# Splitting the attention's score products into quarters, preparing the first block of the next layer during the attention, and reordering the last rows

## The chip, the core and the metric

The kernel runs on one core of a Trainium2 chip. The metric is the device time of one launch in microseconds (us), and the median over several runs is compared.

A core has several engines that run at the same time, each with a queue of its own that it works off strictly in order: PE (TensorE, the matrix products, with its weight loads shown as PEld), DVE (VectorE), ACT (ScalarE), POOL (GpSimd) and SP (SyncE, which here only issues DMA transfers). They wait for each other by semaphores. PE writes its results to a small memory, PSUM, from which DVE or ACT must take them before the place can be written again.

## What is computed

Three layers in a row. The attention has 4 batches and 8 heads, a sequence of 576 and a head dimension of 64; scores that lie more than `tau` below the largest of their row are dropped. Then come two dense layers on 2304 tokens:

```python
scores = scale * np.matmul(q, k.transpose(0, 1, 3, 2))
thresh = np.max(scores, axis=-1, keepdims=True) - tau
scores = np.where(scores >= thresh, scores, -1000000000.0)
attn = exp(scores - max);  attn = attn / (sum(attn) + 1e-09)
x = matmul(attn, v)                       # heads side by side: 2304 x 512
x = ((x @ w_a) * (x @ w_b)) @ w_out       # 512 -> 1536 -> 512
h = x @ w_in                              # 512 -> 1024
solu = h * softmax(h);  ln = (solu - mean) / sqrt(var + 1e-06) * g_ln
out = ln @ w_out2                         # 1024 -> 512
```

## The kernel before

**Order by hand.** The program is written under a manual schedule: each engine gets its instructions in the order in which the Python code emits them, and semaphores are added for every dependence. So the place of a line in the code is its place in its engine's queue.

**Attention (lines 236 to 510).** The 8 heads of each batch are taken in pairs: 16 pairs. A pair has 9 sets of 128 rows of scores (`NS`): 8 full ones and one that holds the last 64 rows of both heads. One step of the loop over `m` (line 430) does two sets, so there are 72 steps with new sets and 6 more that empty the pipeline. In a step the letters of `PROG` give the order. `A` and `B` compute one set each: the products on PE (`scores`, line 280), the row maximum on DVE (line 293) and the exponential on ACT (line 305). `V` multiplies earlier, already transposed weights with `v` (`pv`, line 361). `F` ends a pair. `T`, `U` and `Y` transpose the two sets of the step before on PE (lines 339, 355, 358), and their copies out of PSUM are put at the end of the step on ACT. `a` and `b` mask the two sets on DVE (line 319), and `f` and `z` are places at which small leftover operations go to DVE: reciprocals, and the conversion of weights for the next layer (`conv_emit`), which goes on at every even `m` and at every `m` from 72.

A set has K = 64 (the head dimension). Its 576 columns are cut into two halves `g`, one in the upper 64 rows of the array and one in the lower, so that the two products run side by side. Each f32 product is issued as two passes. A full set is 4 matmul instructions, with 128 columns of weights each. The set of the last 64 rows is 8 instructions on quarters of the array (64 rows by 64 columns).

**The next layer (`moe1`, line 527).** The 2304 tokens are cut into 5 blocks: 4 of 512 tokens, one a batch, and one of 256. A unit is a pair of a block `j` and a slice `f` of 128 hidden columns: `ab` (line 538) computes 24 products of 512 columns into a `ps` buffer, of which there are two, and takes them out by ACT (line 555) and DVE (line 556). Two units later `yacc` adds 12 products. Between the units stand the weight conversion and the preparation of the next block.

**Preparation of a block.** `load_x` (line 182) issues the transfers of the attention's output `xr`, of the reciprocals `zr` and of the small `vs`. `prep_x` (line 197) with `st=0` normalises by four instructions of 512 columns on DVE (line 210) and copies the high part by two of 1024 columns on ACT (line 211); with `st=1` it subtracts to get the low part by two of 1024 columns on DVE (line 213) and orders the store `xsd` (line 215). For block 0 `load_x` stands at `m` = 62, and `prep_x` at the head of the steps 71 and 72 (lines 431 to 434), in front of their scores.

**The last layer (`moe2`, line 638).** 18 tiles of 128 tokens. `hid` (line 649) does 24 products and then a chain over DVE, ACT and POOL (lines 660 to 677) whose result `e` is transposed by `lnt` (line 682): 8 transposes on PE, then twice a multiplication on DVE (line 693), a copy of the high part on ACT (line 694) and a subtraction for the low part (line 695), which is on POOL but for the last tile. `outp` (line 700) does 24 products on the result. In the last step (t = 17) the code emits `hid(17)`, `lnt(16)`, `outp(15)`, the first half of `outp(16)`, `lnt(17)`, the rest of `outp(16)` and `outp(17)`.

Of the kernel before, what the change touches and what calls it, by code (L numbers as in the profile page):

```python
# [8 lines left out]
F32 = mybir.dt.float32  # L9
# [4 lines left out]
AF = mybir.ActivationFunctionType  # L14
ALU = mybir.AluOpType
AX = mybir.AxisListType
PSUM = bass.MemoryType.PSUM
P = 128
# [3 lines left out]
def kernel(  # L22
# [65 lines left out]
    xs = {}  # L88
    vs = {}
    vnew = []  # L90
    later = []
    xhs = [xh_p, None]
    wst = {}
# [88 lines left out]
    def load_x(j):  # L182
        n = LEN[j]
        xr = xr_p.tile([P, KC, NB], F32, name="xr0")[:, :, 0:n]
        zr = xr_p.tile([P, KC, NB], F32, name="zr")[:, :, 0:n]
        for b, s0, m, c in BLK[j]:
            nc.sync.dma_start(out=xr[:, :, c:c + m], in_=xd[b][:, :, s0:s0 + m])
            if b not in vs:
                vs[b] = xr_p.tile([P, KC, 2], F32, name="vs", bufs=B)
                nc.sync.dma_start(out=vs[b], in_=xd[b][:, :, S:S + 2])  # L190
                vnew.append(b)
            for h in range(2):
                zs = rzd[b].rearrange("(k h) s -> h k s", h=2)[h:h + 1, :, s0:s0 + m]
                nc.sync.dma_start(out=zr[h * D:(h + 1) * D, :, c:c + m], in_=zs.to_broadcast([D, KC, m]))
        xs[j] = (xr, zr, xhs[j % 2].tile([P, KC, 2, NB], F32R, name="xt")[:, :, :, 0:n])

    def prep_x(j, st):
        xr, zr, xt = xs[j]
        if st == 0:
            while vnew:  # L200
                b = vnew.pop()
                nc.vector.tensor_scalar(out=vs[b], in0=vs[b], scalar1=neg, scalar2=EPS / S, op0=ALU.mult, op1=ALU.mult)
        for c in range(0, KC, 2):
            k = slice(c, c + 2)
            x0 = xr[:, k]
            if st == 0:
                for e in range(c, c + 2):
                    for b, _, m, o in BLK[j]:
                        xe = xr[:, e, o:o + m]
                        nc.vector.scalar_tensor_tensor(out=xe, in0=xe, scalar=vs[b][:, e, 0:1], in1=zr[:, e, o:o + m], op0=ALU.add, op1=ALU.mult)  # L210
                nc.scalar.activation(out=xt[:, k, 0, :], in_=x0, func=AF.Copy)
            else:
                nc.vector.tensor_tensor(out=xt[:, k, 1, :], in0=x0, in1=xt[:, k, 0, :].bitcast(F32), op=ALU.subtract)
        if st == 1:
            later.append(lambda: nc.sync.dma_start(out=xsd[j], in_=xr))
            xs[j] = xt

    def load_x2(j):
        n = LEN[j]
# [16 lines left out]
    def attention():  # L236
# [43 lines left out]
        def scores(i, s):  # L280
            q, k = ld[i]
            ps = ps_s.tile([P, 2, 512], F32, name="ps")
            qc, h = divmod(s, 2)
            parts = [(slice(0, P), h, slice(qc * P, (qc + 1) * P), 0)] if s < 2 * NQ else [(slice(u * D, (u + 1) * D), u, slice(SM, S), u * D) for u in range(2)]
            for rows, u, c, o in parts:
                for g in range(2):
                    r = slice(g * D, (g + 1) * D)
                    nc.tensor.matmul(ps[rows, g, 0:HS], lhsT=q[r, u, c], rhs=k[r, u, o:o + HS], start=True, stop=True, skip_group_check=True)  # L288
            st[i, s] = ps

        def soft_max(i, s, nm):
# [134 lines left out]
                        conv_emit(wstage, "APD", 2)  # L426

        conv_at = [x for x in range(6, tot // 2 + 6) if x % 2 == 0 or x >= tot // 2]
        PROG = 'ABtVFTUYaufbz'
        for m in range(tot // 2 + 6):  # L430
            if m == tot // 2 - 10:
                load_x(0)
            if 0 <= m - tot // 2 + 1 < 2:
                prep_x(0, m - tot // 2 + 1)
            cur = [divmod(n, NS) for n in (2 * m, 2 * m + 1) if n < tot]
            old = [divmod(n, NS) for n in (2 * m - 2, 2 * m - 1) if 0 <= n < tot]
            lo_old, lo_q = lo_q, []
            pvs = [(j,) + PV[j % 2][m - j * NS // 2] for j in range(max(0, 2 * m // NS - 2), min(NP, 2 * m // NS + 1)) if m - j * NS // 2 in PV[j % 2]]
            mms = [f for p in pvs for f in pv(*p)]
            nm = {}  # L440
            th = {}

            def score(k):
                if k < len(cur):
                    nm[k] = sm.tile([P, 1], F32, name="nm")
                    scores(*cur[k])
                    soft_max(*cur[k], nm[k])
                    soft_exp(*cur[k])

            def thr(k):  # L450
                if k < len(cur):
                    th[k] = soft_thr(nm[k])

            def mask(k):
                if k < len(cur):
                    soft_mask(*cur[k], th[k])
                    if cur[k][1] == NS - 1:
                        recip(cur[k][0])

            def turn(k):  # L460
                if k < len(old):
                    tpose(*old[k])

            for ch in PROG:
                if ch in "AB":
                    score("AB".index(ch))
                elif ch == "V":
                    for mm in mms:
                        mm()
                elif ch == "F":  # L470
                    for j in range(NP):
                        if m - j * NS // 2 == 9:
                            finish(j)
                elif ch in "TU":
                    turn("TU".index(ch))
                elif ch == "Y":
                    for c in old:
                        tpose_tail(*c)
                elif ch in "tu":
                    thr("tu".index(ch))  # L480
                elif ch in "ab":
                    mask("ab".index(ch))
                elif ch == "f":
                    fill(1)
                elif ch == "z":
                    fill(max(1, len(lo_old)))
            for fn in dma_q + later:
                fn()
            dma_q.clear()
            later.clear()  # L490
            i, s = divmod(2 * m, NS)
            r = m - (i * NS + 1) // 2
            if i < NP and r == 0:
                load_v(i)
                if i + 2 < NP:
                    alloc_qk(i + 2)
                    load_k(i + 2)
                    load_q(i + 2)
            for fn in pv_q + evac_q:
                fn()  # L500
            evac_q, pv_q = [], []
            if m in conv_at:
                conv_emit(wstage, "AP", 3)
                conv_load(wstage)
# [22 lines left out]
    def moe1(wp2, ps_t):  # L527
# [9 lines left out]

        def ab(j, f):
            n = LEN[j]
            xt = xs[j]  # L540
            wt = wst[f]
            ps = ps_s.tile([P, 2, 512], F32, name="ps")
            o = []
            for m in range(2):
                pa = ps[:, m]
                k = 0
                for kc in range(KC):
                    for wi, xi in ((0, 0), (0, 1), (1, 0)):
                        nc.tensor.matmul(pa[:, 0:n], lhsT=wt[:, m, wi, kc * P:(kc + 1) * P], rhs=xt[:, kc, xi, :], start=(k == 0), stop=(k == 3 * KC - 1))  # L549
                        k += 1  # L550
                o.append(pa[:, 0:n])
            a32 = gp.tile([P, NB], F32, name="a32")[:, 0:n]
            g32 = gp.tile([P, NB], F32, name="g32")[:, 0:n]
            gt = gp.tile([P, 2, NB], F32R, name="gt", bufs=2 + LAG)[:, :, 0:n]
# [83 lines left out]
    def moe2(ps_t):  # L638
# [7 lines left out]

        s1 = {}

        def hid(t):
            y = yt.pop(t)  # L650
            ph = ps_s.tile([P, 2, 512], F32, name="ps")
            for g in range(2):
                k = 0
                for kc in range(KC):
                    for a, b in ((0, 0), (0, 1), (1, 0)):
                        nc.tensor.matmul(ph[:, g, :], lhsT=y[:, a, kc, :], rhs=w2(2 * kc + g, b), start=(k == 0), stop=(k == 3 * KC - 1))  # L656
                        k += 1
            nm = sm.tile([P, 1], F32, name="nm")
            z = sm.tile([P, 3], F32, name="z2")
            nc.vector.tensor_reduce(out=nm, in_=ph, axis=AX.XY, op=ALU.max, negate=True)  # L660
# [21 lines left out]
        def lnt(t):  # L682
            c, rs = s1.pop(t)
            lt = xh_p.tile([P, 2, NJ, P], F32R, name="lt", tag="xt") if t % 2 else hp.tile([P, 2, NJ, P], F32R, name="lt", bufs=1)
            for g in range(2):
# [6 lines left out]
                l32 = wstage.tile([P, NJ // 2, P], F32, name="l32", tag="w32")  # L692
                nc.vector.tensor_tensor(out=l32, in0=pl, in1=gb, op=ALU.mult)  # L693
                nc.scalar.activation(out=lt[:, 0, gj], in_=l32, func=AF.Copy)  # L694
                (nc.vector if t == NTILE - 1 else nc.gpsimd).tensor_tensor(out=lt[:, 1, gj], in0=l32, in1=lt[:, 0, gj].bitcast(F32), op=ALU.subtract)  # L695
            s2[t] = (lt, rs)

        pos = {}
# [22 lines left out]
        for t in range(NTILE):  # L721
            if t + 2 < NTILE:
                load_y(t + 2, yp)
            if t + 1 < NTILE:
                split_y(t + 1, yp)
            hid(t)
            if t == NTILE - 1:
                lnt(t - 1)
            if 0 <= t - 2:
                outp(t - 2)  # L730
            if 0 <= t - 1 < NTILE - 2:
                lnt(t - 1)
# [76 lines left out]
```

## Time and profile before

| | |
|---|---|
| three runs | 959.18, 957.45, 958.80 us |
| median | 958.8 us |
| the profiled execution | 959.81 us, of which its span (first to last instruction) is 958.0 us |
| PE busy in the span | 938.0 us, 98% |
| DVE busy | 542.0 us, 57% |
| ACT busy | 441.3 us, 46% |
| POOL busy | 196.3 us, 20% |

A busy PE isn't PE at its best: the ends of its instructions are modelled, and one matmul in the pipeline overlaps the next. So gaps and distances between starts are read, not busy time. [...] In the timeline, equal instructions that follow one another are merged into one line. Its columns are: start, length, engine, line of the kernel, operation, result and operands, shape, count, and in brackets the idle time before it with what ended that. The attention covers about the first 278 us, `moe1` goes to about 732 us, and `moe2` to the end.

### The profile page before, as it was taken

To read this page: it belongs to the slowest core of one execution; us is meant where nothing else is said; L and a number is where in the kernel's file an instruction comes from. 1 tells how busy PE (TensorE), PEld (TensorE's weight loads), DVE (VectorE), ACT (ScalarE), POOL (GpSimd) and SP (SyncE) were. 2 spreads that over 40 slices of the span, in tenths; PEclk is the share of its full clock that TensorE was granted. 3 is DMA by queue.
4 is the path that set the end of the run, shared out by engine and by line. 5 is a ranking of instruction groups with operands and counts; after the bars stand their busy time and mean duration, and the time that the engine had idled before them with its cause. 6 is when DMAs were issued, how large, how long until landed. Compare 5 with 4: busy or idle time off the path is not lost.

```text
span 958.0 us, 14042 instructions
## 1 busy us (share of the span) xinstructions
PE 938.0 (98%) x5168; PEld 719.2 (75%) x5168; DVE 542.0 (57%) x1165; ACT 441.3 (46%) x793; POOL 196.3 (20%) x294
## 2 busy tenths in 40 slices
PE   7999999999999999999999999999999999999997
PEld 4656565665667888889888888889988788888885
DVE  6898989889975763223246762222265544444442
ACT  5788887888853451213225532111232433333332
POOL 1112221212221220000013420000022433333331
PEclk9999999999999999999999999999999999999999
DMA  6343343447245563133115541022062111111100
GB/s 176 120 127 112 122 140 102 120 128 199 71 136 154 182 205 75 61 94 132 45 44 199 182 169 67 24 87 78 11 198 66 34 45 44 44 45 44 44 23 34
DMA packets 52612, 95.39 MB, mean 100 GB/s; under 512 B 12736, under 2 KB 28736, under 8 KB 49984
## 3 DMA queue, kind: packets, MB, share of 16 engines
q1 hardware_dynamic: 52112, 93.91, 31.4%
q8 instruction: 41, 0.67, 0.3%
q10 hardware_dynamic: 432, 0.59, 0.2%
q14 instruction: 27, 0.22, 0.1%
HBM read 70.80 MB, written 23.68 MB: 99 GB/s over the span
## 4 chain that ended last, share of the span: by engine, by line
PE 66%; DVE 2%; DMA 2%; ACT 1%; POOL 0%; issue 0%; SPq 0%; ACTq 0%; DVEq 0%
PE ps L549 29%; PE py L572 15%; PE po L708 10%; PE ps L656 9%; PE pl L689 2%; DMA wraw<-in_w_dram 1%; DMA rzd<-zt 0%; POOL lt L695 0%; DVE e L664 0%; ACT e L663 0%; DVE nm L660 0%; ACT ps L668 0%; DVE g L556 0%; DVE e L667 0%; DVE l L693 0%
## 5 line engine op out<-in xcount | busy, mean ns | idle before, releaser
L549 PE MATMUL ps<-xt,w 128*128 128x512 f32 (+1 forms) x1440 | 311.6, 372 | 2.0 <-DVE g L556 2.0
L549 PEld LDWEIGHTS ps<-xt,w 128*128 128x128 f32 x1440 | 253.0, 189 | 51.9 <-DVE g L556 2.4
L144 POOL TENSOR_TENSOR w<-w,w 128x512 fp32r<-128x512 f32 x52 | 77.9, 1497 | 420.2 <-ACT w L141 420.2
L572 PE MATMUL py<-gt,w 128*128 128x512 f32 (+1 forms) x720 | 159.8, 371 | 0.0
L572 PEld LDWEIGHTS py<-gt,w 128*128 128x128 f32 x720 | 126.5, 188 | 24.7
L556 DVE TENSOR_TENSOR g<-ps,a 128x512 f32<-128x512 f32 (+1 forms) x60 | 38.2, 637 | 188.1 <-ACT a L555 188.1
L555 ACT ACTIVATE a<-ps 128x512 f32<-128x512 f32 (+1 forms) x60 | 33.2, 553 | 186.6 <-PE ps L549 183.4
L305 ACT ACTIVATE pe<-ns,nm 128x576 f32<-128x576 f32 x128 | 93.9, 774 | 48.3 <-DVE ns L293 48.1
L319 DVE SCALAR_TENSOR_TENSOR pe<-ns,th,pe 128x576 f32<-128x576 f32 x128 | 102.7, 815 | 16.3 <-ACT pe L305 12.5
L293 DVE TENSOR_SCALAR_CACHE_REDUCE ns<-ps 128x576 f32<-128x576 f32 x144 | 102.6, 749 | 10.7 <-PE ps L288 10.4
L708 PE MATMUL po<-w,lt 128*128 128x512 f32 x432 | 103.6, 395 | 2.7 <-ACT lt L694 1.4
L656 PE MATMUL ps<-w,ys 128*128 128x512 f32 x432 | 104.6, 397 | 1.5 <-POOL ys L524 1.4
L288 PE MATMUL ps<-k,q 64*128 64x288 f32 (+1 forms) x640 | 96.2, 439 | 5.0 <-DMA k<-in_qkv_dram 5.0
L708 PEld LDWEIGHTS po<-w,lt 128*128 128x128 f32 x432 | 81.7, 190 | 21.7 <-ACT lt L694 2.2
L656 PEld LDWEIGHTS ps<-w,ys 128*128 128x128 f32 x432 | 80.0, 188 | 19.6 <-POOL ys L524 1.8
L332 ACT ACTIVATE pt<-tp 128x512 f32<-128x512 f32 (+1 forms) x160 | 78.1, 545 | 1.7 <-PE tp L339 1.4
L310 POOL TENSOR_SCALAR th<-nm,toff 128x1 f32<-128x1 f32 x144 | 38.4, 268 | 188.0 <-DVE ns L293 188.0
L370 PE MATMUL po<-pt,vr 128*64 128x322 f32 (+1 forms) x512 | 76.6, 420 | 0.0
L339 PEld LDWEIGHTS tp<-ident,pe 128*128 128x128 f32 x512 | 56.4, 143 | 26.5 <-issue 14.4
L339 PE MATMUL tp<-ident,pe 128*128 128x128 f32 x512 | 71.6, 280 | 3.3 <-ACT pt L332 2.8
L288 PEld LDWEIGHTS ps<-k,q 64*128 64x128 f32 (+1 forms) x640 | 48.2, 178 | 30.2 <-issue 9.5
L660 DVE TENSOR_REDUCE nm<-ps 128x1 f32<-128x1024 f32 x18 | 22.0, 1224 | 70.0 <-PE ps L656 70.0
(72 smaller groups left out, 820.7 us busy)
## 6 DMA issues: line engine op xcount, KB each, us to landing
wraw<-in_w_dram SPq DMA_DIRECT2D x36, 512.0 KB
q<-in_qkv_dram SPq DMA_DIRECT2D x15, 576.0 KB
k<-in_qkv_dram SPq DMA_DIRECT2D x30, 176.0 KB
xd<-xp SPq DMA_DIRECT2D x16, 289.0 KB
y<-yd SPq DMA_DIRECT2D x18, 256.0 KB
vr<-in_v_dram SPq DMA_DIRECT2D x16, 256.0 KB
xr<-xd SPq DMA_DIRECT2D x4, 1024.0 KB
zr<-rzd SPq DMA_DIRECT2D x8, 512.0 KB
```

The source lines that it names most:

```text
L144: nc.gpsimd.tensor_tensor(out=w["o"][1], in0=w["f"] if wide else raw, in1=w["o"][0].bitcast(F32), op=ALU.subtract)
L288: nc.tensor.matmul(ps[rows, g, 0:HS], lhsT=q[r, u, c], rhs=k[r, u, o:o + HS], start=True, stop=True, skip_group_check=True)
L293: nc.vector.tensor_scalar(out=ns, in0=st[i, s][:, :, 0:HS], scalar1=-SCALE, scalar2=None, op0=ALU.mult, op1=ALU.min, accum_out=nm)
L305: nc.scalar.activation(out=pe.rearrange("p (g s) -> p g s", g=2), in_=ns, func=AF.Exp, bias=nm, scale=-1.0)
L319: nc.vector.scalar_tensor_tensor(out=pv, in0=ns, scalar=th, in1=pv, op0=ALU.is_le, op1=ALU.mult, accum_out=z[:, s:s + 1])
L332: evac_q.append(lambda: nc.scalar.activation(out=out, in_=in_, func=AF.Copy))
L339: nc.tensor.transpose(tp[:, kc, :], pe[:, o:o + P], ident)
L370: nc.tensor.matmul(po[h * D:(h + 1) * D], lhsT=lhsT, rhs=rhs, start=(kc == 0), stop=(kc == NQ), skip_group_check=True)
L549: nc.tensor.matmul(pa[:, 0:n], lhsT=wt[:, m, wi, kc * P:(kc + 1) * P], rhs=xt[:, kc, xi, :], start=(k == 0), stop=(k == 3 * KC - 1))
L572: nc.tensor.matmul(py, lhsT=wt[:, 2, wi, oc * P:(oc + 1) * P], rhs=gt[:, gi, :], start=(first and k == 0), stop=(last and k == 2))
L656: nc.tensor.matmul(ph[:, g, :], lhsT=y[:, a, kc, :], rhs=w2(2 * kc + g, b), start=(k == 0), stop=(k == 3 * KC - 1))
L708: nc.tensor.matmul(po, lhsT=lt[:, a, j, :], rhs=w2(2 * KC + j, b), start=(k == 0), stop=(k == 3 * NJ - 1))
```

## The change

- `scores`: a full set is no longer 2 products with 128 columns of weights in two passes, but 4 with 64 columns each, on quarters of the array, as the set of the last rows was before.
- `load_x(0)` is emitted at `m` = 30 instead of 62. `prep_x(0, ...)` is no longer called at `m` = 71 and 72. In its place `prep_slots` cuts the same work into pieces of 512 columns (4 norms, 4 high parts, 4 low parts) in 8 slots, and one slot is emitted at `z`, after the second mask, of each odd `m` from 37 to 51. The ACT part goes to the end of the list of copies of that step. `vs` moves to another pool.
- The products of `ab(0, 0)` are emitted at `m` = 72 after `Y` (`X` in `PROG`), in front of the last products with `v`. Their way out of PSUM stays in `moe1`.
- `moe2`: the DVE, ACT and POOL part of `hid` becomes `chain`, called after `hid(t)`, but in the last step only after `lnt(16)`. The low part of tile 16 goes to DVE, like that of tile 17.

```diff
@@ prep_slots, ab_mm (new) @@
+    def prep_slots(j):
+        xr, zr, xt = xs[j]
+        def norm(e):
+            while vnew:
+                b = vnew.pop()
+                nc.vector.tensor_scalar(out=vs[b], in0=vs[b], scalar1=neg, scalar2=EPS / S, op0=ALU.mult, op1=ALU.mult)
+            for b, _, m, o in BLK[j]:
+                xe = xr[:, e, o:o + m]
+                nc.vector.scalar_tensor_tensor(out=xe, in0=xe, scalar=vs[b][:, e, 0:1], in1=zr[:, e, o:o + m], op0=ALU.add, op1=ALU.mult)
+        def high(e):
+            nc.scalar.activation(out=xt[:, e, 0, :], in_=xr[:, e], func=AF.Copy)
+        def low(e):
+            nc.vector.tensor_tensor(out=xt[:, e, 1, :], in0=xr[:, e], in1=xt[:, e, 0, :].bitcast(F32), op=ALU.subtract)
+            if e == KC - 1:
+                later.append(lambda: nc.sync.dma_start(out=xsd[j], in_=xr))
+                xs[j] = xt
+        slots = []
+        for c in range(0, KC, 2):
+            slots += [(lambda e=e: norm(e), lambda e=e: high(e)) for e in range(c, c + 2)]
+            slots += [(lambda e=e: low(e), None) for e in range(c, c + 2)]
+        return slots
+    def ab_mm(j, f):
...
@@ scores @@
-            parts = [(slice(0, P), h, slice(qc * P, (qc + 1) * P), 0)] if s < 2 * NQ else [(slice(u * D, (u + 1) * D), u, slice(SM, S), u * D) for u in range(2)]
-            for rows, u, c, o in parts:
+            parts = [(h, qc * P + u * D, 0) for u in range(2)] if s < 2 * NQ else [(u, SM, u * D) for u in range(2)]
+            for t, (u, c0, o) in enumerate(parts):
+                c = slice(c0, c0 + D)
                 for g in range(2):
                     r = slice(g * D, (g + 1) * D)
-                    nc.tensor.matmul(ps[rows, g, 0:HS], lhsT=q[r, u, c], rhs=k[r, u, o:o + HS], start=True, stop=True, skip_group_check=True)
+                    nc.tensor.matmul(ps[t * D:(t + 1) * D, g, 0:HS], lhsT=q[r, u, c], rhs=k[r, u, o:o + HS], start=True, stop=True, skip_group_check=True)
@@ the loop over m @@
-        PROG = 'ABtVFTUYaufbz'
+        PROG = 'ABtVFTUYXaufbz'
-            if m == tot // 2 - 10:
+            if m == 30:
                 load_x(0)
-            if 0 <= m - tot // 2 + 1 < 2:
-                prep_x(0, m - tot // 2 + 1)
+                x_slots = prep_slots(0)
...
+                elif ch == "X":
+                    if m == tot // 2:
+                        pre[0, 0] = ab_mm(0, 0)
                 elif ch == "z":
                     fill(max(1, len(lo_old)))
+                    if m >= 37 and m % 2 and x_slots:
+                        norm_low, high = x_slots.pop(0)
+                        norm_low()
+                        if high:
+                            evac_q.append(high)
@@ ab @@
+            o = pre.pop((j, f)) if (j, f) in pre else ab_mm(j, f)
@@ moe2 @@
+            ph_of[t] = ph
+        def chain(t):
+            ph = ph_of.pop(t)
...
-                (nc.vector if t == NTILE - 1 else nc.gpsimd).tensor_tensor(out=lt[:, 1, gj], in0=l32, in1=lt[:, 0, gj].bitcast(F32), op=ALU.subtract)
+                (nc.vector if t >= NTILE - 2 else nc.gpsimd).tensor_tensor(out=lt[:, 1, gj], in0=l32, in1=lt[:, 0, gj].bitcast(F32), op=ALU.subtract)
...
             hid(t)
             if t == NTILE - 1:
                 lnt(t - 1)
+            chain(t)
```

## Rows read from the trace of the kernel before

**Rows 1.** Stretches: bounds, length, each engine's busy time (count), granted clock, DMA share, GB/s

```profile
20.00:265.00 245.00, 243.49 (x1862) 148.34 (x1858) 220.66 (x607) 199.19 (x383) 49.14 (x145) 1.00 0.42 125
...
272.00:274.00 2.00, 2.00 (x10) 1.85 (x10) 2.00 (x4) 1.37 (x5) 0.00 (x0) 0.50 0.10 41
274.00:276.00 2.00, 2.00 (x16) 1.69 (x16) 1.90 (x6) 1.02 (x3) 0.00 (x0) 0.75 0.01 2
```

**Rows 2.** Waits of DVE and PE from 20 to 265 us: total us, times, longest

```profile
DVE ns L293 <- PE ps L288: 6.7, 12, 0.8
...
PE tq L355 <- ACT zt L396: 1.4, 3, 0.5
```

**Rows 3.** Timeline of the weight loads around three steps of the attention

```profile
150.25 0.21 PEld L288 LDWEIGHTS ps<-k,q 64*64 64x64 f32 x8 [0.17 <-DVE ns L293]
150.90 0.30 PEld L288 LDWEIGHTS ps<-k,q 64*128 64x128 f32 x4 [0.44 <-issue]
151.59 0.63 PEld L370 LDWEIGHTS po<-pt,vr 128*64 128x64 f32 x8 [0.38 <-ACT xp L378]
...
153.68 0.79 PEld L288 LDWEIGHTS ps<-k,q 64*128 64x128 f32 x8 [0.17 <-issue]
154.85 0.20 PEld L370 LDWEIGHTS po<-pt,vr 128*64 128x64 f32 x4 [0.38 <-issue]
```

**Rows 4.** Instructions of the tile `xr`, then of line 144: duration in ns, least, median, most

```profile
L210 DVE SCALAR_TENSOR_TENSOR xr<-xr,vs,zr x4: 740/748/1769, 265.1 to 268.2; 128x512 f32<-128x512 f32 x4
...
L213 DVE TENSOR_TENSOR xt<-xr,xt x2: 1218/1220/1221, 272.2 to 273.4; 128x1024 fp32r<-128x1024 f32 x2
...
L144 POOL TENSOR_TENSOR w<-w,w x11: 1275/1282/1289, 53.9 to 244.2; 128x512 fp32r<-128x512 f32 x11
```

**Rows 5.** Timeline of the end of the attention

```profile
265.13 3.76 DVE L210 SCALAR_TENSOR_TENSOR xr<-xr,vs,zr 128x512 f32<-128x512 f32 x4
...
268.82 0.75 DVE L293 TENSOR_SCALAR_CACHE_REDUCE ns<-ps 128x576 f32<-128x576 f32 x1
...
269.31 0.28 PE L391 MATMUL rt<-ident,rz 128*9 128x128 f32 x1
...
271.85 1.12 PE L339 MATMUL tp<-ident,pe 128*128 128x128 f32 x4 [2.27 <-ACT pt L332]
...
277.68 1.17 PE L549 MATMUL ps<-xt,w 128*128 128x512 f32 x4
```

**Rows 6.** Timeline of the way from the attention's last copies to the fifth unit of `moe1`

```profile
283.44 0.25 ACT L396 ACTIVATE zt<-rt 9x128 f32<-9x128 f32 x1
...
286.83 0.60 ACT L555 ACTIVATE a<-ps 128x512 f32<-128x512 f32 x1 [3.14 <-DMA rzd<-zt]
...
305.89 0.43 DVE L131 TENSOR_SCALAR wlow<-wraw 128x512 uint32<-128x512 uint32 x1 [7.17 <-DMA wraw<-in_w_dram]
...
307.81 7.40 PE L549 MATMUL ps<-xt,w 128*128 128x512 f32 x24 [1.99 <-DVE g L556]
```

**Rows 7.** Timeline of the last two tiles

```profile
931.88 1.23 DVE L660 TENSOR_REDUCE nm<-ps 128x1 f32<-128x1024 f32 x1 [4.30 <-PE ps L656]
932.47 5.71 PE L708 MATMUL po<-w,lt 128*128 128x512 f32 x24
...
935.89 0.76 DVE L667 TENSOR_SCALAR e<-e,mu 128x1024 f32<-128x1024 f32 x1
...
938.19 1.29 DVE L693 TENSOR_TENSOR l<-pl,gl 128x512 f32<-128x512 f32 x2
...
944.76 1.04 PE L689 MATMUL pl<-ident,e 128*128 128x128 f32 x8
945.47 0.69 DVE L693 TENSOR_TENSOR l<-pl,gl 128x512 f32<-128x512 f32 x1 [5.99 <-PE pl L689]
945.55 8.43 PE L708 MATMUL po<-w,lt 128*128 128x512 f32 x36
...
948.85 0.69 DVE L695 TENSOR_TENSOR lt<-l,lt 128x512 fp32r<-128x512 f32 x1 [0.70 <-ACT lt L694]
```

More of the change, by code (lines that the diff above doesn't have):

```diff
@@ L90 @@
     vnew = []
+    pre = {}
     later = []
@@ L188, in load_x @@
             if b not in vs:
-                vs[b] = xr_p.tile([P, KC, 2], F32, name="vs", bufs=B)
+                vs[b] = const.tile([P, KC, 2], F32, name=f"vs{b}")
                 nc.sync.dma_start(out=vs[b], in_=xd[b][:, :, S:S + 2])
@@ L216, in prep_x @@
             xs[j] = xt
+    def prep_slots(j):
[20 more added lines that the diff above has]
+    def ab_mm(j, f):
+        n = LEN[j]
+        xt = xs[j]
+        wt = wst[f]
+        ps = ps_s.tile([P, 2, 512], F32, name="ps")
+        o = []
+        for m in range(2):
+            pa = ps[:, m]
+            k = 0
+            for kc in range(KC):
+                for wi, xi in ((0, 0), (0, 1), (1, 0)):
+                    nc.tensor.matmul(pa[:, 0:n], lhsT=wt[:, m, wi, kc * P:(kc + 1) * P], rhs=xt[:, kc, xi, :], start=(k == 0), stop=(k == 3 * KC - 1))
+                    k += 1
+            o.append(pa[:, 0:n])
+        return o
     def load_x2(j):
@@ L539, in ab @@
             n = LEN[j]
[L540 to L551, printed above, removed]
+            o = pre.pop((j, f)) if (j, f) in pre else ab_mm(j, f)
             a32 = gp.tile([P, NB], F32, name="a32")[:, 0:n]
@@ L647, in moe2 @@
         s1 = {}
+        ph_of = {}
         def hid(t):
```

## The prediction

> **What bounds the kernel now.** I first read the stretches for granted clock and idle time, then the waits, then the timeline where PE waits long. From 20 to 265 us, 67 of the attention's 72 steps of 3.66 us each, PE waits for others 1.4 us in all [rows 2]. The transposes, scores and products follow one another with the same distances in step after step, so PE sets the pace. DVE is almost as full: of 245 us it is busy 220.7 [rows 1], most of the rest goes with the wait for the exponential in each step, which the change leaves, and only 6.7 us are waits for the scores of PE [rows 2]. That 6.7 us is all the room that DVE has. After the attention PE has three long waits that the change may touch: one at its end [rows 5], one at the fifth unit of `moe1` [rows 6] and one in the last two tiles [rows 7].
>
> **Quarters.** The price is read from the distance between the first weight load of a set and the first of what follows. A set of quarters takes 150.90 - 150.25 = 0.65 us and a full set as it is now 151.59 - 150.90 = 0.69, each with a change of the array's division before and after it. Two full sets in a row take 154.85 - 153.68 = 1.17, so the second, without such a change, takes 0.48 [rows 3]. All sets being quarters, a step takes 0.65 + 0.48 = 1.13. Of the 72 steps 56 now have two full sets, and gain 0.04 each: 2.2 us. In 16 steps a full set stands beside one of quarters, 0.69 + 0.65 = 1.34, and these gain 0.21 each: 3.4 us. Together 5.6 us less on PE, 5.2 of them in the 67 steps. What no row shows is a third pass of quarters in a row. Its weights must load behind the pass before. In the one set shown all eight loads, those of the second pass too, lie within 0.21 us [rows 3], while a pass lasts 0.48 / 2 = 0.24, so I take it as hidden. The bound on the other side is that the quarters gain nothing.
>
> [...]
>
> **Preparation moved to m = 37 to 51.** It adds to DVE four norms of 0.75 us, four low parts of half of 1.22 us [rows 4] and the small scaling of 0.23 at the first: 5.7 us in 15 steps. It is put behind the second mask, so the next step's row maximum is queued behind it, then the exponential, and then the transposes on PE a step later. Those 15 steps take 55 us and hold 22% of DVE's room, 1.5 us. So they grow by 5.7 - 1.5 = 4.2 us. On ACT it adds four copies of half of 1.06, behind the copies of each step; ACT is busy 199 of 245 us [rows 1], and I cost that at nothing (if ACT were full, 2.1 us). The other 52 steps can gain 52/72 of 5.6, or 4.0 us, and the room of DVE there, 5.2, is larger. Because the two engines now run nearly level and a step has either the one or the other ahead, I take 3.2 of it. Attention: 4.2 - 3.2 = **+1.0 us**. The bounds: if all of DVE's room could be used, 5.7 - 6.7 = -1.0; if no room and no gain of the quarters were had, +5.7.
>
> `load_x(0)` brings five transfers to SP's queue about 32 steps earlier. The transfer engines are 42% busy in the stretch [rows 1]; the transfers of queries and keys that come to stand behind them are for pairs two ahead, about 33 us, and the norms come seven steps, 25 us, after the issue. So nothing is waited for; a cost would be a late first norm. The store `xsd` moves earlier with the last low part. The other pool for `vs` costs nothing.
>
> **The end of the attention.** Now the four norms hold DVE from 265.13 until the row maximum of step 71 starts at 268.82, 3.7 us. Behind it come the exponentials and, behind these on ACT, the copies that free PSUM for the transposes. PE ends its work at 269.6 and waits 2.27 us for such a copy, until 271.85 [rows 5]. After it the granted clock is 0.50 from 272 to 274 and 0.75 from 274 to 276 [rows 1], so that half of 2 us and a quarter of 2 us are lost: 1.5. Without the norms the maximum could start up to 3.7 us earlier; I take 3.4, as its scores come a little after 265.13. The copy then ends at 271.85 - 3.4 = 268.4, ahead of PE's 269.6. The wait goes, and the clock stays: **-3.8 us**. The bounds: -2.3, if the clock falls all the same, and -3.8. What is late next is none of the step's own chain, which then has over 1 us to spare.
>
> **The products of `ab(0, 0)` earlier.** The 24 products, 5.5 us, are the same work on PE, in front of the last 20 products with `v` in place of behind them. Queued behind them are these products, then the copies `zt` on ACT and the store of the reciprocals. The first copy of `moe1` comes 3.14 us after `zt` and waits for that store [rows 6], and on that copy hangs the later conversion of weights, its transfers, and the wait of PE at 307.81. Now PE is done with the attention at 277.68 [rows 5], but `zt` runs only at 283.44 [rows 6], held on ACT behind the weight conversion. That is 5.8 us of cover. In the new order PE reaches the end of the attention at 277.68 - 3.8 + 5.5 = 279.4, `zt` at 279.7, and the chain is 3.7 us earlier: the same as PE. DVE's conversion in front of `zt` starts over 5 us earlier (norms and low parts are gone from there) and is done by then. So this edit costs and gives nothing, and the wait of 2.0 us at 307.81 with its slow clock (24 products in 7.40 us [rows 6], against 5.5) stays: **0**, between -3.9, if this wait went, and +1.
>
> **The last two tiles.** Now DVE works off the whole chain of tile 17, from 931.88, before it comes to the rows of tile 16, at 938.19. PE goes through the 24 products from 932.47 at 0.23 each (36 in 8.43), is done at 938.0, and then waits for the low part on POOL and runs at a lower clock until the transposes of tile 17 at 944.76 [rows 7]. In the new order the four DVE operations of tile 16 start at 932.4, when its transposes are done. The same four of tile 17 took 945.47 to 949.54, 4.07 us [rows 7], so they end at 936.5, before PE asks at 938.0. PE does its 12 products until 940.8. The chain of tile 17 starts at 936.5 in place of 931.88; `e` came 4.77 us after that start (935.89 + 0.76), so it is ready at 941.3. PE waits 0.5 us, transposes for 0.8, and does the next 12 products until 944.9. DVE starts on tile 17's rows 1.54 us after `e` (938.19 - 936.65), at 942.8; the low parts are ready at 944.9 and 946.9, when PE asks for them at 945.3 and 947.7. The last 24 products end at 950.4, against 945.55 + 36 x 0.23 = 953.8: **-3.4 us**. The bounds: -4.0, all that PE loses there now, and -2.4, if the 0.5 us of waiting were followed by a slow clock for 2 us.
>
> **The sum.** +1.0 - 3.8 + 0 - 3.4 = -6.2 us. The profiled execution took 959.8 us (its span 958.0), so it would be 953.6. The median is 1.0 below that execution, and I predict 958.8 - 6.2 = **952.6**.
>
> **The rivals.**
> - *The attention pays little.* DVE's room is used across steps and the first term is -1.0, or the wait at 307.81 shrinks so that the clock stays up after it (-2 or more). For it: DVE and PE lag each other by up to a step through the two `ps` buffers. Against it: DVE's waits for PE are 12 in 67 steps, so most steps have no room. -8.2 to -10: about 949.5.
> - *The quarters don't pay.* PE is faster, but DVE keeps the pace of before everywhere, or third passes are slower; the first term is 4.2 to 5.7. -3.0 to -1.5: 955.8 to 957.3. For it: DVE has 6.7 us of room in all.
> - *The wait at the end stays*, since DVE, now behind PE, gives the last masks late; then only the tail and the first term count: -2.4, 956.4. Against it: the spare time of over 1 us.
> - *Slower: DVE and POOL hold each other up in the slots.* One of the four norms took 1.77 us in place of 0.75 [rows 4], beside a subtraction of line 144 on POOL. Were each of the 8 slots so, the preparation would take 14.4, the first term would be 14.4 - 1.5 - 3.2 = +9.7, and the time 958.8 + 9.7 - 7.2 = 961.3. It decides from a slot of 1.5 us on, where the gains are used up. Against it: the 11 subtractions between 20 and 265 us all took 1.28 [rows 4]; they start early in a step, behind a copy that ends the step before, and the slots stand at its end.
>
> [...]
>
> **How the numbers follow.** A difference of 0.2%, 1.9 us, is about what a measurement of this kernel can tell from no change. The chances: the forecast 0.56 (its own range 951 to 954.8), the attention pays little 0.17, the quarters don't pay 0.15, the wait stays 0.06, slower 0.06. Faster by over 1.9 us, below 956.9, are the first two and most of the next two: 0.88. Within it 0.06, slower 0.06. The range leaves out the slower rival and the ends of the others: 947.5 to 957.3.
>
> **What would show it.** After the change: the rows of a step have one weight load in place of two forms, and a step's two sets take 1.13; DVE waits less for PE from 20 to 265, and PE waits for DVE around the slots; the granted clock is 1.00 at the end of the attention and the wait for a copy there is gone; the fifth unit still waits about 2 us; the wait in front of the half `outp(16)` is gone and a short one stands in front of the transposes of tile 17. I am wrong if steps with slots grow by clearly more than 0.3 us on average, if third passes of quarters stand further apart than 0.24 us, or if the first copy of `moe1` isn't about 3.7 us earlier than the attention's own shift leaves it.

## The result

The changed kernel takes 945.9 us (median of 944.22 to 947.54), 0.987 of the kernel before on the same chip, 95% interval [0.985, 0.9891]. That is 12 us less, twice what was forecast, and below the range. The profiled execution took 945.94 us, its span is 944.1 against 958.0.

The end of the attention, as the timeline of the changed kernel shows it (answers to [rows 5, 6]; columns as there):

```profile
266.19 1.20 PE L332 MATMUL ps<-k,q 64*64 64x288 f32 x16
...
266.97 0.76 DVE L337 TENSOR_SCALAR_CACHE_REDUCE ns<-ps 128x576 f32<-128x576 f32 x1
267.32 1.08 PE L414 MATMUL po<-pt,vr 128*64 128x256 f32 x8
...
270.92 0.60 PE L383 MATMUL tp<-ident,pe 128*128 128x128 f32 x4
...
272.37 5.74 PE L256 MATMUL ps<-xt,w 128*128 128x512 f32 x24
...
281.35 0.25 ACT L440 ACTIVATE zt<-rt 9x128 f32<-9x128 f32 x1
...
284.39 0.60 ACT L595 ACTIVATE a<-ps 128x512 f32<-128x512 f32 x1 [2.79 <-DMA rzd<-zt]
```

The transposes of the last step (270.92) no longer wait, and the 24 products of `ab(0, 0)` follow at 272.37. The granted clock, given as a share of full speed, stays at 1.00, as the stretches of the changed kernel show (answer to [rows 1], same columns):

```profile
20.00:265.00 245.00, 239.19 (x2315) 138.39 (x2311) 222.61 (x609) 197.84 (x382) 49.16 (x145) 1.00 0.43 129
...
272.00:274.00 2.00, 2.00 (x13) 1.57 (x12) 1.90 (x4) 2.00 (x6) 0.27 (x1) 1.00 0.07 13
274.00:276.00 2.00, 2.00 (x11) 1.65 (x10) 1.76 (x2) 0.31 (x2) 1.32 (x1) 1.00 0.85 268
```

The way to the fifth unit of `moe1` and a later stretch of the same timeline (the first lines answer to [rows 6]):

```profile
302.91 0.43 DVE L132 TENSOR_SCALAR wlow<-wraw 128x512 uint32<-128x512 uint32 x1 [6.63 <-DMA wraw<-in_w_dram]
...
304.83 5.74 PE L256 MATMUL ps<-xt,w 128*128 128x512 f32 x24 [1.88 <-DVE g L596]
...
342.22 0.43 DVE L132 TENSOR_SCALAR wlow<-wraw 128x512 uint32<-128x512 uint32 x1 [7.06 <-DMA wraw<-in_w_dram]
...
345.30 1.90 PE L612 MATMUL py<-gt,w 128*128 128x512 f32 x7 [2.09 <-ACT y L616]
```

The wait at the fifth unit is still 1.88, but the 24 products behind it take 5.74, not 7.40. A second wait of the same kind, 2.09 us at 345.30, is new. The last two tiles (answers to [rows 7]):

```profile
922.06 8.42 PE L754 MATMUL po<-w,lt 128*128 128x512 f32 x36
...
925.96 1.22 DVE L706 TENSOR_REDUCE nm<-ps 128x1 f32<-128x1024 f32 x1
...
930.87 1.06 PE L735 MATMUL pl<-ident,e 128*128 128x128 f32 x8 [0.39 <-DVE rz L716]
931.69 8.43 PE L754 MATMUL po<-w,lt 128*128 128x512 f32 x36
```

PE's 36 products from 922.06 run through, and the transposes of tile 17 wait 0.39.

What no step of the prediction had stands in the middle of `moe1`. Three units in a row, first of the kernel before, then of the changed one (timeline; the distance between two starts of line 549 or 256 is a whole unit of 24 + 12 products, with nothing waiting):

```profile
401.26 5.74 PE L549 MATMUL ps<-xt,w 128*128 128x512 f32 x24
406.84 2.95 PE L572 MATMUL py<-gt,w 128*128 128x512 f32 x12
409.63 5.73 PE L549 MATMUL ps<-xt,w 128*128 128x512 f32 x24
...
418.00 2.21 PE L549 MATMUL ps<-xt,w 128*128 128x512 f32 x9
```

```profile
397.16 5.60 PE L256 MATMUL ps<-xt,w 128*128 128x512 f32 x24
402.60 2.88 PE L612 MATMUL py<-gt,w 128*128 128x512 f32 x12
405.32 5.60 PE L256 MATMUL ps<-xt,w 128*128 128x512 f32 x24
...
413.48 5.60 PE L256 MATMUL ps<-xt,w 128*128 128x512 f32 x24
```

The same instructions on the same shapes, at a granted clock of 1.00 in both (from 396 to 420 us): 8.37 us a unit before, 8.16 after, or 232.5 and 226.7 ns a product. Taken over all 512-column units (the mean distance of starts within a unit, its median over the four blocks), the products of `ab` stand 232.3 to 232.7 ns apart at f = 0 to 4, 227 to 228 at f = 5 to 8 and 232.7 to 232.8 at f = 9 to 11 in the kernel before, and 226.7 to 227.3 at every f after. The units of the 256-column block gain nothing: 4.28 to 4.33 us before, 4.31 or 4.32 after.

Where the 13.9 us of the two spans lie, from the start of one marker to the next in each timeline:

| stretch | before | after | difference | forecast |
|---|---|---|---|---|
| to the scores of step 5 | 22.32 | 21.46 | -0.9 | 0 |
| to the scores of step 71 | 242.17 | 244.73 | +2.6 | +1.0 |
| to the first copy of `moe1` | 22.33 | 18.20 | -4.1 | -3.8 |
| to the fifth unit | 20.98 | 20.44 | -0.5 | 0 |
| to the first product of `hid(0)` | 424.52 | 419.08 | -5.4 | 0 |
| to the first of `hid(17)` | 193.69 | 191.80 | -1.9 | 0 |
| to the last of `outp(17)` | 27.58 | 24.03 | -3.6 | -3.4 |

The first row is chance: kernels that start alike have 21.2 to 22.3 there. The three terms of the forecast give -5.1 together, against -6.2. The three stretches that it left at nothing give -7.8.

### The profile page after: what moved, and what is told of

It reads as the page before. It is cut to its first block, busy times and chain, and to the rows that moved or that the text cites. A ratio compares the mean times of both kernels' runs of the same rounds, so it can differ in the third digit from the quotient of the medians.

```text
span 944.1 us, 15070 instructions
## 1 busy us (share of the span) xinstructions
PE 921.9 (98%) x5680; PEld 704.0 (75%) x5680; DVE 542.4 (57%) x1169; ACT 440.4 (47%) x795; POOL 192.6 (20%) x292
## 4 chain that ended last, share of the span: by engine, by line
PE 60%; DVE 3%; DMA 3%; ACT 2%; issue 1%; SPq 0%; POOL 0%; ACTq 0%; DVEq 0%
PE ps L256 26%; PE py L612 14%; PE po L754 10%; PE ps L698 9%; DMA wraw<-in_w_dram 2%; PE pl L735 2%; DVE g L596 1%; ACT gt L597 0%; DVE e L710 0%; DVE w L138 0%; ACT e L709 0%; DVE nm L706 0%; DVE xr L211 0%; ACT w L128 0%; ACT a L595 0%
## 5 line engine op out<-in xcount | busy, mean ns | idle before, releaser
L256 PE MATMUL ps<-xt,w 128*128 128x512 f32 (+1 forms) x1440 | 305.8, 368 | 1.9 <-DVE g L596 1.9
L612 PE MATMUL py<-gt,w 128*128 128x512 f32 (+1 forms) x720 | 157.5, 368 | 2.1 <-ACT y L616 2.1
L698 PE MATMUL ps<-w,ys 128*128 128x512 f32 x432 | 102.6, 393 | 1.6 <-POOL ys L575 1.4
L754 PE MATMUL po<-w,lt 128*128 128x512 f32 x432 | 101.4, 390 | 0.7 <-POOL lt L741 0.6
L332 PE MATMUL ps<-k,q 64*64 64x288 f32 x1152 | 91.2, 424 | 4.7 <-DMA k<-in_qkv_dram 4.4
L414 PEld LDWEIGHTS po<-pt,vr 128*64 128x64 f32 x512 | 32.7, 136 | 42.5 <-issue 17.2
L332 PEld LDWEIGHTS ps<-k,q 64*64 64x64 f32 x1152 | 36.8, 134 | 32.8 <-DVE ns L337 7.8
```

What stands on the lines that cost most here:

```text
L332: nc.tensor.matmul(ps[t * D:(t + 1) * D, g, 0:HS], lhsT=q[r, u, c], rhs=k[r, u, o:o + HS], start=True, stop=True, skip_group_check=True)
L414: nc.tensor.matmul(po[h * D:(h + 1) * D], lhsT=lhsT, rhs=rhs, start=(kc == 0), stop=(kc == NQ), skip_group_check=True)
L612: nc.tensor.matmul(py, lhsT=wt[:, 2, wi, oc * P:(oc + 1) * P], rhs=gt[:, gi, :], start=(first and k == 0), stop=(last and k == 2))
L754: nc.tensor.matmul(po, lhsT=lt[:, a, j, :], rhs=w2(2 * KC + j, b), start=(k == 0), stop=(k == 3 * NJ - 1))
```

## Experiments

Two theories for the faster products. **Placement:** taking `vs` out of the pool `xr` moves, by the kernel's own memory layout, the first five weight buffers (`wp`) up by 128 bytes in each partition, since `const` grows by 128 and `xr` shrinks by as much. The blocks `xt`, the tiles `gt` and the other four weight buffers stay. Before, the five began at 32 modulo 256 bytes (17184, 29472, ...) and all the others at 160 (113568, 203680, 129952, ...); after, all begin at 160. The units with f = 0 to 4 and 9 to 11 use the five, those with f = 5 to 8 the other four. **History:** the products are faster because of what runs elsewhere (the quarters, the clock kept up at the end of the attention).

**`vs` alone**, in the kernel before:

```diff
-                vs[b] = xr_p.tile([P, KC, 2], F32, name="vs", bufs=B)
+                vs[b] = const.tile([P, KC, 2], F32, name=f"vs{b}")
```

> The kernel before with one edit: the four small vs tiles (32 bytes a partition each) are taken from the constants in place of the pool xr. This moves the first five weight buffers of the next layers by 128 bytes and leaves the blocks xt where they were. Theory A (placement: a product runs at 227 ns a start or at 232 depending on where its weights lie against the other operand): the 24 products of a unit take 5.44 us in place of 5.58 in nearly all units, and the time falls by 7 us (5 to 9), to about 951. Theory B (history: the quarters or the clock that didn't fall leave PE in a faster rhythm): no change, 958.3. The prediction's step (another pool costs nothing) agrees with B.

0.9916 of before, [0.9888, 0.9943]: 8.0 us from an edit that moves 128 bytes. Its units, in the timeline:

```profile
397.98 5.60 PE L549 MATMUL ps<-xt,w 128*128 128x512 f32 x24
403.42 2.88 PE L572 MATMUL py<-gt,w 128*128 128x512 f32 x12
406.14 5.60 PE L549 MATMUL ps<-xt,w 128*128 128x512 f32 x24
```

8.16 us, as in the changed kernel, without quarters and with the slow end of the attention. **The reverse**, the changed kernel with `vs` back in `xr`:

> The changed kernel with the vs tiles back in the pool xr, so that the first five weight buffers lie where they did before. Theory A: about 7 us slower than the changed kernel, 953 (951 to 955), which is the predicted 952.6 without the placement. Theory B: as the changed kernel, 946.

0.9955, [0.9933, 0.9977], and the units are slow again:

```profile
400.01 5.74 PE L256 MATMUL ps<-xt,w 128*128 128x512 f32 x24
405.58 2.95 PE L612 MATMUL py<-gt,w 128*128 128x512 f32 x12
408.37 5.73 PE L256 MATMUL ps<-xt,w 128*128 128x512 f32 x24
```

So all the rest of the change is worth 4.3 us (2.2 to 6.4), and the history theory falls: quarters and clock are here, the fast products aren't.

**Is it the place itself or the distance?** In the kernel before, an unused `const` tile of 128 bytes moves everything behind it together:

```diff
     gl = const.tile([P, NJ], F32, name="gl")
+    pad = const.tile([P, 32], F32, name="pad")
+    nc.gpsimd.memset(pad, 0.0)
```

> The kernel before with an unused tile of 128 bytes a partition in the constants: all weight buffers, blocks and results move by 128 bytes together. If only the address of the weights counts: the units with weights in the first five buffers get the short distance (227 ns) and those in the other four lose it, 958 minus about 3. If the distance between weights and block counts: the same as before unit by unit, 958.3. If neither counts (theory B): 958.3 as well, but then e1 doesn't move either.

1.0009, [0.9989, 1.003], and the distances between products are those of before at every f (232 to 233, 227 to 228, 232.7). What counts is the distance between the weights and the other operand. Half of it, 64 bytes, by two of the four `vs` tiles in `const`:

```diff
-                vs[b] = xr_p.tile([P, KC, 2], F32, name="vs", bufs=B)
+                vs[b] = const.tile([P, KC, 2], F32, name=f"vs{b}") if b < 2 else xr_p.tile([P, KC, 2], F32, name="vs", bufs=2)
```

> The kernel before with only two of the four vs tiles in the constants: the first five weight buffers move by 64 bytes, to a distance of 64 bytes from the place of the blocks within 256, in place of 128 before and 0 in e1. If only the same place within 256 bytes is free of the cost: 957 and 232 ns a start. If the cost goes with the distance: about 954 and 229 ns. If 64 bytes are harmless: 950 and 227 ns.

0.9952, [0.9933, 0.9972]. The units stand between the two, 8.24 us or 229 ns a product, so the cost goes with the distance there. In `hid`, where the weight buffers hold the streamed operand, the 64 bytes gain nothing: 232.5 ns, against 232.0 in the kernel before. Why isn't known.

```profile
399.40 5.66 PE L549 MATMUL ps<-xt,w 128*128 128x512 f32 x24
404.89 2.91 PE L572 MATMUL py<-gt,w 128*128 128x512 f32 x12
407.64 5.66 PE L549 MATMUL ps<-xt,w 128*128 128x512 f32 x24
```

**Without touching `vs`**, an unused tile between the pools `xr` and `xh` moves the blocks and the other four buffers away from the five. 128 bytes (n = 32) make the distance 0 modulo 256, 256 bytes (n = 64) make it 128 again:

```diff
     xr_p = ctx.enter_context(tc.tile_pool(name="xr", bufs=1))
+    gap = ctx.enter_context(tc.tile_pool(name="gap", bufs=1)).tile([P, n], F32, name="gap")
+    nc.gpsimd.memset(gap, 0.0)
```

> The kernel before with an unused tile of 128 bytes a partition between the pools xr and xh: `vs`, the first five weight buffers, xr0, zr and ys stay where they were, and the blocks xt, gt and the other four weight buffers move up by 128 bytes, so that the first five stand at the same place as the blocks modulo 256 bytes. Placement theory (the distance between weights and block modulo 256 bytes counts): as e1_vs_const, 0.9916 of before, about 950; products of all units 226.8 ns apart. Rival (it is `vs` itself, its transfers or its neighbours that counted): 1.000, about 958, products of the first five units still 231.7 ns apart. Rival (blocks must stand at 160 modulo 256): the units of the other four buffers get slower too, above 958.

> The same with an unused tile of 256 bytes in that place: the distance is 128 bytes modulo 256 as in the kernel before. Placement modulo 256: as before, 1.000, products of the first five units 231.7 ns apart. Rival (the distance counts modulo 512 or by another power): another distance between the products than 231.7.

0.9943, [0.9925, 0.9961], and 1.002, [1.0004, 1.0036]. The units of the first, then of the second:

```profile
399.15 5.60 PE L551 MATMUL ps<-xt,w 128*128 128x512 f32 x24
404.59 2.88 PE L574 MATMUL py<-gt,w 128*128 128x512 f32 x12
407.31 5.60 PE L551 MATMUL ps<-xt,w 128*128 128x512 f32 x24
```

```profile
399.71 5.74 PE L551 MATMUL ps<-xt,w 128*128 128x512 f32 x24
405.28 2.95 PE L574 MATMUL py<-gt,w 128*128 128x512 f32 x12
408.07 5.73 PE L551 MATMUL ps<-xt,w 128*128 128x512 f32 x24
```

8.16 and 8.36. That is the placement theory, with nothing else changed but the unused tile. The products of `hid` say the same once more: in the kernel with the gap of 128 bytes only the first of the 18 tiles, whose tokens lie in the pool `xr` that didn't move, keeps 232 ns (median), and the other tiles have 227. The first kernel gains 5.5 us where `vs` alone gained 8.0, with intervals that overlap: in its profile PE waits 2.9 us at the fifth unit and the products behind the wait are slow (24 in 7.37 us), which in the profile of `vs` alone they aren't. The second is 0.2% slower than before; nothing here explains that.

In the next four the ratios lie close to the changed kernel's 0.987, and but for the last one the intervals overlap with its own; what an edit is worth is read from the traces.

**The quarters undone** in the changed kernel (the old `parts` and loop in `scores`):

```diff
-            parts = [(h, qc * P + u * D, 0) for u in range(2)] if s < 2 * NQ else [(u, SM, u * D) for u in range(2)]
+            parts = [(slice(0, P), h, slice(qc * P, (qc + 1) * P), 0)] if s < 2 * NQ else [(slice(u * D, (u + 1) * D), u, slice(SM, S), u * D) for u in range(2)]
```

> The changed kernel with full sets of scores as before (two products of 128 columns in place of four of 64); all else is kept. The prediction's sum: the quarters are worth 3.2 to 5.6 us of the attention, so 949 to 951.5. The rival that the quarters don't pay: 946. Theory B says that the distance in the next layers goes back to 232 ns as well, 954 or more; theory A says that it stays at 227.

0.9888, [0.9854, 0.9923]; its products stand 226.7 ns apart, so here too the history theory fails. **The preparation at its old place** (no slots at `z`):

```diff
-            if m == 30:
+            if m == tot // 2 - 10:
                 load_x(0)
-                x_slots = prep_slots(0)
+            if 0 <= m - tot // 2 + 1 < 2:
+                prep_x(0, m - tot // 2 + 1)
```

> The changed kernel with block 0 prepared as before: its transfers at step 62, its norms, copies and low parts at the heads of steps 71 and 72. Quarters, early products, tail and placement are kept. The prediction's steps: the slots cost 4.2 us less what others gain, and undoing them brings back the wait of 2.3 us with its slow clock (1.5) at the end of the attention. So steps 37 to 51 get faster by up to 4.2, the end slower by 3.8: 945.5 to 947. If the slots are hidden for nothing (rival): 949.7. If the wait at the end doesn't come back because the early products of the next layer fill it: 942.

0.9899, [0.9878, 0.992]. The attention of these, from the start of one step's scores to another's (us):

| | steps 5 to 36 | 36 to 52 | 52 to 71 |
|---|---|---|---|
| before | 113.61 | 58.55 | 70.01 |
| changed | 112.32 | 62.26 | 70.15 |
| no quarters | 113.62 | 62.14 | 70.56 |
| preparation late | 112.30 | 58.41 | 69.50 |

The quarters give 1.3 us in the first 31 steps and little afterwards, and the slots cost 3.85 where they stand (62.26 - 58.41). With the preparation late, the wait at the end of the attention is there again, and the slow clock (granted 0.50 from 270 to 274) falls on the early `ab(0, 0)`:

```profile
269.29 1.11 PE L383 MATMUL tp<-ident,pe 128*128 128x128 f32 x4 [2.77 <-ACT pt L376]
...
272.03 7.47 PE L256 MATMUL ps<-xt,w 128*128 128x512 f32 x24
```

From the scores of step 71 to `hid(0)` this kernel takes 462.90 us, the changed one 457.72. So in these two profiles the new place of the preparation costs 4.56 up to step 71 and gives 5.2 behind it, nearly nothing in sum.

**The early products undone:**

```diff
-        PROG = 'ABtVFTUYXaufbz'
+        PROG = 'ABtVFTUYaufbz'
```

> The changed kernel without the early products: ab(0, 0) is computed in the next layer, as before. The prediction's step: it costs and gives nothing, 945.9, with the copy zt and so the first copy of the next layer up to 2 us earlier, since the products with v no longer stand behind it; then the wait at the fifth unit gets shorter by as much and the time falls to 944. The other way: the early products cover the copies out of PSUM at the end of the attention, and without them PE waits there, by up to 1.5 us: 947.5.

0.9891, [0.9866, 0.9917]. The way from step 71 to the first copy of `moe1` is 284.12 - 266.42 = 17.70 without them and 18.20 with them: the edit brings nothing there. **The old order of the last tiles:**

```diff
-            if t == NTILE - 1:
-                lnt(t - 1)
-            chain(t)
+            chain(t)
+            if t == NTILE - 1:
+                lnt(t - 1)
...
-                (nc.vector if t >= NTILE - 2 else nc.gpsimd).tensor_tensor(out=lt[:, 1, gj], in0=l32, in1=lt[:, 0, gj].bitcast(F32), op=ALU.subtract)
+                (nc.vector if t == NTILE - 1 else nc.gpsimd).tensor_tensor(out=lt[:, 1, gj], in0=l32, in1=lt[:, 0, gj].bitcast(F32), op=ALU.subtract)
```

> The changed kernel with the last two tiles in the order of before (the chain of tile 17 ahead of the rows of tile 16, whose low part is on POOL). The prediction's step: 3.4 us slower, 949.3 (2.4 to 4.0), all of it between the start of outp(16) and the transposes of tile 17.

0.9918, [0.9896, 0.994]. From the start of `hid(17)` to the last product it takes 27.66 us against 24.03, and the waits of [rows 7] are back:

```profile
931.36 0.73 PE L754 MATMUL po<-w,lt 128*128 128x512 f32 x2 [1.44 <-ACT lt L740]
...
932.71 4.00 PE L754 MATMUL po<-w,lt 128*128 128x512 f32 x10 [0.62 <-POOL lt L741]
936.50 1.23 PE L735 MATMUL pl<-ident,e 128*128 128x128 f32 x8
```

Part of this is not certain to come. The ten products take 4.00 us here, at a granted clock of 0.50 from 934 to 936. In the profile of `vs` alone, which has the old order too, the same waits are followed by ten products in 2.56 us, at a granted clock of 1.00:

```profile
930.37 0.73 PE L708 MATMUL po<-w,lt 128*128 128x512 f32 x2 [1.44 <-ACT lt L694]
931.73 2.56 PE L708 MATMUL po<-w,lt 128*128 128x512 f32 x10 [0.62 <-POOL lt L695]
```

From `hid(17)` to the last product that profile takes 26.07, and the one with the gap of 256 bytes 26.22. So the old order costs 2.0 to 2.2 us more than the new one where the clock stays up, and 3.6 where it falls.

**A faster version.** My reading of the two waits for weights in `moe1` was that they come behind `load_x`, whose transfers (four in the trace, the expectation says five) stand in SP's queue ahead of a weight transfer. In the changed kernel the four are issued from 288.62 to 291.73, and the next weight transfer at 291.85. So `load_x(1)` is moved into the attention (and its `xt` is taken when it is first written):

```diff
+            if m == 60:
+                load_x(1)
...
-                if n == 0:
-                    load_x(1)
```

> The changed kernel with load_x(1) emitted at m = 60 of the attention in place of the first unit of moe1. My reading is that PE's wait of 1.9 us at the fifth unit (304.83) comes from the weight transfer that stands behind the five transfers of load_x(1). By it the wait shrinks to below 0.5 and the kernel gains 1.5 to 2: 0.998 of the changed kernel, 0.985 of before, about 944. Rival (the transfer is late because the conversion itself starts late): the wait stays at 1.9, the time as that of the changed kernel.

941.7 us, 0.9847 of before, [0.9831, 0.9864]. That is 2.2 us less than the changed kernel's 0.987 would give beside it; the two were measured apart and their intervals overlap, so the gain is read from the trace. The fifth unit comes 2.0 us earlier, without a wait:

```profile
300.09 2.88 PE L617 MATMUL py<-gt,w 128*128 128x512 f32 x12
...
302.81 3.56 PE L259 MATMUL ps<-xt,w 128*128 128x512 f32 x15
```

The second wait, which I had left alone, is gone too: the products that waited at 345.30 run through at 340.89. Why that one went wasn't tested. **The low parts of the slots on POOL**, on top of that:

```diff
-            nc.vector.tensor_tensor(out=xt[:, e, 1, :], in0=xr[:, e], in1=xt[:, e, 0, :].bitcast(F32), op=ALU.subtract)
+            nc.gpsimd.tensor_tensor(out=xt[:, e, 1, :], in0=xr[:, e], in1=xt[:, e, 0, :].bitcast(F32), op=ALU.subtract)
```

> As e10_load1_early, and the four low parts of block 0 in the slots of the attention are subtracted on POOL in place of DVE. Theory that the slots cost what DVE's work is beyond its room: 2.4 us less for DVE, the 16 steps from m = 36 to 51 shrink from 62.3 to about 60 us, and the kernel is 2.0 to 2.4 below e10, about 942. Rival (POOL and DVE shut each other out, or the order of the slots costs): those steps stay at 62 or more, no gain.

0.9869, [0.9855, 0.9884]: slower than the kernel it was built on, 943.5 to 944.5 us beside 941.4 to 942.2. The steps 36 to 52 take 63.77 in place of 62.24. The groups of DVE and POOL from 133 to 199 us (columns: line, engine, operation, operands, shape, count, busy us, mean ns, idle before), one line without and two with the low parts on POOL:

```profile
L366 DVE SCALAR_TENSOR_TENSOR pe<-ns,th,pe 128x576 f32<-128x576 f32 x30 | 24.1, 815 | 4.2 <-ACT pe L352 2.8 <-POOL th L357 1.4
```

```profile
L366 DVE SCALAR_TENSOR_TENSOR pe<-ns,th,pe 128x576 f32<-128x576 f32 x29 | 26.3, 915 | 4.7 <-ACT pe L352 2.6 <-POOL th L357 2.1
...
L237 POOL TENSOR_TENSOR xt<-xr,xt 128x512 fp32r<-128x512 f32 x4 | 6.1, 1527 | 0.0
```

DVE got rid of four low parts, 2.7 us, and its masks grew by 29 x 0.10 = 2.9. The mean hides what happens: 30 of the 33 masks from 133 to 199 us still take 0.80 to 0.82 us, and the three that start while one of these subtractions runs on POOL take 1.69 to 1.83. One of them, in the timeline:

```profile
166.55 1.26 POOL L237 TENSOR_TENSOR xt<-xr,xt 128x512 fp32r<-128x512 f32 x1
166.62 1.81 DVE L366 SCALAR_TENSOR_TENSOR pe<-ns,th,pe 128x576 f32<-128x576 f32 x1 [0.16 <-POOL th L357]
```

So the two engines are in each other's way where these two meet: 1.81 us for the mask against 0.82, and 1.26 to 1.80 for POOL's four subtractions.

## Why the prediction was wrong

**The step that failed** is the clause "The other pool for `vs` costs nothing". It rested on no row and had no bound, and it carried two thirds of the gain. Its price is the difference of two traces, the changed kernel and the one with `vs` back, which both have the second wait (2.09 and 2.10 us) and no slow products behind the first: 419.08 against 425.41 us from the fifth unit to `hid(0)`, and 191.80 against 193.69 from there to `hid(17)`, where the products of `hid` go from 232.0 to 227.3 ns. Together that is -8.2, beside the -8.0 that `vs` alone measured. With the clock that no longer falls at the fifth unit (-1.7) and the new wait at 345.30 (+2.1) this makes -7.8, where the table has -7.3 for these two stretches. The rows for a doubt were there: the kernel before does the same product in 232 to 233 ns at eight of the twelve f and in 227 to 228 at the other four. I read those distances as one price.

**The attention:** +2.6 in place of +1.0. The slots were sized nearly right, 3.7 to 3.85 against 4.2. The term that failed is the gain of the other steps: 1.15 (113.61 + 70.01 - 112.32 - 70.15) against 3.2. The price of the quarters holds where nothing waits, 267.32 - 266.19 = 1.13 for a step's two sets, and in them the third and fourth passes start 0.24 us behind the one before, as forecast. But PE's gain turned into waits. The rival "the quarters don't pay" foresaw such a loss, but from DVE's pace or the third passes; these waits are for ACT. The waits from 20 to 265 us of the changed kernel (answer to [rows 2]):

```profile
DVE ns L337 <- PE ps L332: 4.8, 7, 0.7
PE tq L399 <- ACT zt L440: 4.1, 5, 1.4
...
PE po L414 <- ACT pt L376: 0.9, 2, 0.6
PE po L414 <- ACT xp L422: 0.7, 2, 0.4
```

PE waits 5.7 us in place of 1.4, for copies that ACT makes, and DVE's waits for PE fell by 1.9 only. Each edit alone brings some of it: PE waits 3.9 us with the slots and without quarters, 2.9 with quarters and the preparation late (both to 262 us). That the steps from 52 on gain 0.5 with the preparation late and nothing with it in the slots stays open.

**The end of the attention:** right, -4.1 for -3.8; the wait is gone and the granted clock is 1.00. **The early products:** right, nothing, and the wait at the fifth unit stayed, 1.88 for "about 2". **Behind that wait** I kept the slow clock; in the changed kernel it doesn't come (granted 1.00 from 304 to 312 us). It isn't the change that decides this: the wait is there in most profiles, and the products behind it are slow in some of them (24 in 7.35 to 7.40 us after 1.99, 2.84 and 2.95 us of waiting, and not after 2.55). **The last tiles:** right in the mechanism, with a wait of 0.39 for the 0.5. That -3.6 came so near to -3.4 is luck in part: both count the slow clock of the old order (granted 0.50), and where it doesn't fall the term is -2.0, outside its bound of -2.4. **The rival of DVE and POOL** didn't come: the four norms took 0.69 to 0.75. It can be made to come by putting POOL's subtractions into the slots (three masks of 1.69 to 1.83 us).

So the sum of what was costed was off by 1.1 us in the profile and by 1.9 in the runs, in both inside its bounds: the changed kernel without the placement measured 0.9955, [0.9933, 0.9977], which is -4.3 us, and -6.2 of 958.8 is 0.9935. The forecast was outside its range because an edit was costed at nothing without looking at what else it moves.

## What to carry to other kernels

An edit that changes the size of a pool moves all that lies behind it: compare the places of the operands, modulo 256 bytes, before calling it free (128 bytes were worth 8.0 us here). When one trace shows the same instruction at the same clock with two durations, ask what the two groups share before pricing anything from it. And work that is moved out of a wait into a loop where two engines run level is not free there: the slots cost 3.85 us here.

## What was not expected of the hardware

In `moe1`, the distance between starts of products with 128 x 128 f32 weights and 512 columns depends on where the weights lie against the other operand: 227 ns where both begin at the same place modulo 256 bytes, 232 to 233 where they are 128 bytes apart, 229 at 64. Shifting both by 128 bytes changed nothing, and a distance of 128 + 128 was as good as 0. `hid` agrees at 0 and at 128 (227 and 232), but not in everything: at 64 it has 232.5, and in the kernel before the 6 of its 24 products that read the unmoved buffers are no faster than the others. So the pace isn't settled for each product alone. Other distances weren't tried, nor what in the chip makes it so.
